# MLP-mixer and grouped attention kernel: w2 copies behind identity and square, slot 1's first layer in a second-layer bank, last weighted sums in column halves

## The chip, the cores and the metric

The kernel runs on one core of one Trainium2 chip, in one launch. The metric is the device time in microseconds, median of the runs. Engines are TensorE (PE; its weight loads are PEld), VectorE (DVE), ScalarE (ACT), GpSimdE (POOL) and SyncE (SP), which issues most DMAs. TensorE writes its products to PSUM, which has eight banks here, each of 128 partitions by 512 float32; the other engines read them out.

## The reference

x has 2048 rows of 448 columns. Two branches read the layer-normalized x, and both are added to x:

```python
xn = _layernorm(x, axis=-1)
return x + _A_ref(xn, A_wq, A_wk, A_wv, A_wo) + _B_ref(xn, B_w1, B_b1, B_w2, B_b2)

# _A_ref: 16 heads of 28 share one key and one value head
q = (x @ wq).reshape(B, S, H, Dh).transpose(0, 2, 1, 3)
k, v = x @ wk, x @ wv
scores = einsum("bhqd,bkd->bhqk", q, k) * (Dh ** -0.5)
o = einsum("bhqk,bkd->bhqd", softmax(scores), v)
return o.transpose(0, 2, 1, 3).reshape(B, S, H * Dh) @ wo

# _B_ref: normalizes once more, then 448 -> 1792 -> 448
y = _layernorm(x, axis=-1)
h = _gelu(einsum("bsd,df->bsf", y, w1) + b1)      # tanh form
return einsum("bsf,fd->bsd", h, w2) + b2
```

## The kernel before

Rows are worked on in four chunks c of 512 (four tiles of 128). The order of the instructions on each engine is written out by hand (the tile framework's manual schedule): generators yield after each matmul, and the loops around them put other work in between. The framework adds the waits. Each engine takes its instructions strictly in that order, so an instruction that waits holds up all behind it.

**Three stages.** To about 66 us: layer norms, projections to q, k and v, query rows stored to DRAM (`qd`). From 66 to about 480 us: the MLP, with the row maxima of the attention scores and the first "turned" scores put in between. Then attention proper, to the end.

**Precision.** Matrices are split into a rounded high part and the remainder (`w1h`, `w1l`; `w2h`, `w2l`; `hh`, `hl`), and a product is three matmuls: high by high, high by low, low by high.

**The MLP in slots.** There are 4 x 14 slots n, one for each chunk c and block ft of 128 of the 1792 hidden columns, and two more to finish. Slot n runs the first layer of block n (`mlp1`, eleven matmuls at lines L179, L182 and L184 into the bank `ph`), and then the second layer of block n - 2 (`mlp2`, twelve matmuls at L625, L628, L631 into four banks `m2_0` to `m2_3`, in which all 14 blocks add up). PSUM is full: three banks `m` for scores, four for the second layer, and only one `ph`.

Behind the first layer follows the gelu. ScalarE reads the bank twice: identity with bias into `hx` (L599) and the scaled square into `hz` (L600); the square's end frees `ph`. GpSimdE makes the tanh's argument (L601, L602). `middle` is ScalarE's tanh (L605) and GpSimdE's last two steps (L606, L607: `hx` is then the gelu). `ending`, which the next slot runs under the name `closing`, rounds it to `hh` on ScalarE (L612) and makes the remainder `hl` on GpSimdE (L614).

These pieces are called between the twelve matmuls of `mlp2`, by a table from the matmul's number to the piece (`stages`). `texp` is an exponential of turned scores (L569). In slots 5, 7, 9, 11, 13 (and so on in later chunks; `norms`) another table also holds the normalization of the next chunk, whose transposes (L271, evacuated to `xh` at L272) use the bank `ph`. Slots 0 and 1 have no `mlp2`: their pieces are called at the slot's end in order of their numbers.

**Splitting w2.** In each odd slot of the first chunk (1, 3, ..., 13) two blocks of w2 are split: `w2_split` at once issues ScalarE's copy into `w2h` (L339), thus ahead of the slot's first layer, identity and square. Its `low` part, a stage, makes `w2l` of one block on VectorE and of the other on GpSimdE (L343), and issues the load of the next raw pair on SP. `w2h` and `w2l` take the space that the projections used, among others for `qe`, from which query rows are stored to `qd` until the MLP begins; the first writes wait for these DMAs.

**Scores in the slots.** After some matmuls a score matmul into an `m` bank is put in: row maxima (L517 on TensorE, reduced by VectorE at L518) or turned scores (L551, read out by VectorE at L552). In the odd slots of the first chunk only row maxima are put in; the even slots begin with four turned ones. There are three `m` banks, so a score matmul waits for VectorE to have read the third one before it.

**The tail.** Attention works in units u (chunk, group of four heads) and key tiles kt. Weighted sums are four matmuls for each kt, one a head, each into 32 partitions of the bank `po` by 512 columns (`pv`, L829). After the last unit's last kt, `end_jobs` runs: nine spins (matmuls of the identity, L396, read by nobody) while VectorE normalizes `po` in two column halves (`shares`: transpose L807, reciprocal L808, transpose L809, product L810), ScalarE and VectorE split the result (`oth` L811, `otl` L812), and TensorE multiplies by the output weights (L741, L742, L743).

Of the kernel before, what the change touches and what calls it, by code (L numbers as in the profile page):

```python
# [15 lines left out]
P = 128  # L16
# [22 lines left out]
def block_kernel(ctx, tc, x, wq, wk, wv, wo, w1, b1, w2, b2, out):  # L39
# [296 lines left out]
    def w2_split(s):  # L336
        raw = wl_q.pop(0)
        ab = slice(2 * s, 2 * s + 2)
        act.activation(w2h[:, ab, :], raw, AF.Copy)  # L339

        def low():
            for eng, b in ((dve, 0), (pool, 1)):
                eng.tensor_sub(w2l[:, 2 * s + b, :], raw[:, b], f(w2h[:, 2 * s + b, :]))  # L343
            if s + 2 < NF // 2:
                w2_load(s + 2)

        return low

    def q_slot(c, i):
        xh, xl = xts[c, False]  # L350
# [43 lines left out]
    def spin(n, t=None):  # L394
        for _ in range(n):
            pe.matmul(idle if t is None else t, ident, ident, start=True, stop=True)  # L396
# [194 lines left out]

    def mlp1(c, ft):
        yh, yl = xts[c, True]
        ph = php.tile([P, CW], F32, name="ph")
        fs = slice(ft * P, (ft + 1) * P)
        yield from proj_steps(ph, lambda b: w1h[:, b, fs], lambda b: w1l[:, b, fs], yh, yl)
        hx = hrp.tile([P, CW], F32, name="hx", bufs=2)
        hz = hrp.tile([P, CW], F32, name="hz", bufs=2)
        act.activation(hx, ph, AF.Identity, bias=b1t[:, ft:ft + 1])  # L599
        act.activation(hz, ph, AF.Square, bias=b1s[:, ft:ft + 1], scale=GELU[0] ** 0.5)  # L600
        pool.tensor_scalar(hz, hz, 1.0, 1.0, op0=ALU.mult, op1=ALU.add)  # L601
        pool.tensor_mul(hz, hz, hx)  # L602

        def middle():
            act.activation(hz, hz, AF.Tanh, scale=GELU[1])  # L605
            pool.tensor_scalar(hz, hz, 0.5, 0.5, op0=ALU.mult, op1=ALU.add)  # L606
            pool.tensor_mul(hx, hx, hz)  # L607

        def ending():
            hh = hrp.tile([P, CW], F32R, name="hh")  # L610
            hl = hrp.tile([P, CW], F32R, name="hl")
            act.activation(hh, hx, AF.Copy)  # L612
            hs[c, ft] = (hh, hl)
            pool.tensor_sub(hl, hx, f(hh))  # L614

        return middle, ending

    def mlp2(c, ft, stages):
        if ft == 0:
            m2s[c] = [m2p.tile([P, D], F32, name=f"m2_{k}") for k in range(CT)]  # L620
        m2 = m2s[c]
        hh, hl = hs.pop((c, ft))
        for k in range(CT):
            ts = slice(k * P, (k + 1) * P)
            pe.matmul(m2[k], hh[:, ts], w2h[:, ft, :], start=(ft == 0), stop=False)  # L625
            stages[3 * k]()
            yield
            pe.matmul(m2[k], hh[:, ts], w2l[:, ft, :], start=False, stop=False)  # L628
            stages[3 * k + 1]()
            yield  # L630
            pe.matmul(m2[k], hl[:, ts], w2h[:, ft, :], start=False, stop=(ft == NF - 1))  # L631
            if ft == NF - 1:
                t = CT * c + k
                a = lines.pop(t)
                dve.tensor_add(a, a, m2[k])
                nc.sync.dma_start(ad[:, t, :], a)
            stages[3 * k + 2]()
            yield

    def slot(n):  # L640
        nonlocal maxed, ending
        middle = low = none
        closing, ending = ending, none
        if n < len(mslots):
            if split(*mslots[n]):
                low = w2_split(n // 2)
            middle, ending = yield from mlp1(*mslots[n])
        texp = turned_exp if n < len(mslots) - 1 else none
        stages = {0: texp, 1: texp, 2: low, 3: closing, 5: middle}
        if n in norms:  # L650
            stages = {4: norms[n], 5: texp, 6: texp, 7: closing, 8: norms[n], 9: middle, 10: low}
        if n >= 2:
            yield from mlp2(*mslots[n - 2], [stages.get(i, none) for i in range(12)])
        else:
            for i in sorted(stages):
                stages[i]()
# [131 lines left out]
        pool.tensor_sub(otl, oc, f(oth))  # L788
        yield

    def end_jobs(u, po):
        while side.step() or oside.step():
            pass
        c, g = units[u]
# [2 lines left out]
        tr, rb, on = att.tile([P, CW], F32, name="tr2", bufs=1), att.tile([P, CW], F32, name="tr", bufs=1), att.tile([P, CW], F32, name="oc", bufs=1)  # L797
        rc = att.tile([P, CW // 32], F32, name="rc", bufs=1)
        last = mtile([P, P])
        spin(9, last)  # L800

        def blocks(t, h):
            return t[:, h].rearrange("p (a b) -> p a b", b=32)
# [17 lines left out]

    pos, ps, pairs = {}, {}, {}

    def pv(u, kt):
        if kt == 0:
            pos[u] = op.tile([P, CW], F32, name="po")
        po = pos[u]
        for j in range(4):
            pe.matmul(po[32 * j:32 * j + 32, :], vs[:, kt, :], ps.pop((u, kt, j)),  # L829
                      start=(kt == 0), stop=(kt == NT - 1))  # L830
        if kt == NT - 1:
            if u == NU - 1:
                end_jobs(u, pos.pop(u))
                return
            side.add(norm_jobs(u, pos.pop(u)))
            side.step()
            c, g = units[u]
            if c < NCH - 1 and g == NG - 1:
                oside.add(o_wait(c, range(NG), range(CT)))
# [36 lines left out]
    for n, (u, kt) in enumerate(steps):  # L876
# [11 lines left out]
        for what in ORDERS[u in TURNED][n % 2]:  # L888
# [21 lines left out]
            elif what == "P":  # L910
                assert not jobs
                for _ in range(BURST if n else 0):
                    pv(*pvq.pop(0))
    while pvq:
        pv(*pvq.pop(0))
    while side.step():
        pass
    while oside.step():
# [24 lines left out]
```

## Time and profile before

| | us |
|---|---|
| median of 3 runs | 1094.62 (1094.16 to 1096.04) |
| profiled execution | 1097.33 |
| its span, first to last instruction | 1095.6 |
| mean granted TensorE clock | 0.996 of full speed |
| TensorE busy | 1080.2 (99%) |
| VectorE busy | 909.2 (83%) |
| ScalarE busy | 736.7 (67%) |
| GpSimdE busy | 561.0 (51%) |

The page has the busy times, the span in 40 equal slices (a digit is a tenth; PEclk is the granted clock of TensorE), the chain of work that ended last, and groups of instructions. The waits view adds up who waited for whom: engine, tile and line, then the releaser; total, times, longest. The timeline view lists instructions in order of time: start, duration, engine, line, operation, output and input tile, and in brackets the idle time before it with what ended that. The windows view gives for a stretch its length, the busy time of TensorE, its weight loads, VectorE, ScalarE and GpSimdE, then the granted clock, the DMA share and GB/s. Tile numbers are left out of names, so `m` stands for score banks and for `m2_0` to `m2_3` alike. TensorE records of float32 matmuls come in pairs, those of the rounded type singly.

### The profile page before, as it was taken

The page shows a single profiled execution, that of the slowest core. Times are in us where ns is not written, and L with a number is a line of the kernel's source. Part 1 is how long each engine was busy: PE and PEld are TensorE (multiplying, and loading weights), DVE is VectorE, ACT ScalarE, POOL GpSimd, SP SyncE. Part 2 cuts the span into 40 slices and gives each one's busy share as a digit, 9 for nine tenths or more (in the row PEclk, how much of TensorE's full clock was granted, in tenths as well). Part 3 has the DMA queues.
Part 4 walks back from the last instruction along what each step waited for, and adds up shares of the span by engine and source line. Part 5 has one row for each costly group of instructions (what it writes and reads, how often), then busy time and mean ns, then how long its engine had stood idle before and what let it go on. Part 6 is the DMA issues. An engine that isn't in the chain of part 4 may idle for free.

```text
span 1095.6 us, 17543 instructions
## 1 busy us (share of the span) xinstructions
PE 1080.2 (99%) x5777; PEld 715.9 (65%) x5777; DVE 909.2 (83%) x1847; ACT 736.7 (67%) x1279; POOL 561.0 (51%) x694
## 2 busy tenths in 40 slices
PE   9989999999999999999999999999999999999998
PEld 8768888888888888865555555555546454555444
DVE  7768899888988998886888997799987898886743
ACT  6765555666666666658777776677775777765783
POOL 6347788768767777764334433433442343343220
PEclk9989999999999999999999999999999999999999
DMA  8675546777877777877977798588796678895720
GB/s 280 206 230 136 137 120 161 196 177 190 209 184 181 192 195 170 216 169 156 204 186 173 182 227 215 129 199 190 181 215 174 174 175 200 199 199 131 182 52 35
DMA packets 140512, 195.15 MB, mean 178 GB/s; under 512 B 17086, under 2 KB 96116, under 8 KB 140420
## 3 DMA queue, kind: packets, MB, share of 16 engines
q1 hardware_dynamic: 127684, 172.11, 62.9%
q0 software_dynamic: 11328, 21.33, 8.7%
q8 instruction: 46, 0.75, 0.3%
q10 hardware_dynamic: 1408, 0.57, 0.2%
q14 instruction: 46, 0.38, 0.1%
HBM read 115.22 MB, written 77.71 MB: 176 GB/s over the span
## 4 chain that ended last, share of the span: by engine, by line
PE 92%; DVE 5%; ACT 1%; issue 1%; DMA 1%; SPq 0%; ACTq 0%; DVEq 0%
PE po L829 22%; PE m L517 18%; PE m L860 17%; PE ph L179 10%; PE m L551 5%; PE m L628 4%; PE m L625 4%; PE m L631 4%; PE m L741 1%; PE ph L182 1%; PE ph L184 1%; PE m L742 1%; PE m L743 1%; DVE mx L518 1%; PE qp L179 1%
## 5 line engine op out<-in xcount | busy, mean ns | idle before, releaser
L518 DVE TENSOR_REDUCE mx<-m 128x1 f32<-128x512 f32 x784 | 506.4, 679 | 80.8 <-PE m L517 71.9
L861 ACT ACTIVATE p<-m 128x512 f32<-128x512 f32 x784 | 402.5, 609 | 163.3 <-PE m L860 163.2
L517 PE MATMUL m<-ks,qm 128*128 128x512 f32 x784 | 322.2, 411 | 0.0
L860 PE MATMUL m<-xh,ks 128*128 128x512 f32 x784 | 258.7, 399 | 0.9 <-DVE half L712 0.9
L829 PE MATMUL po<-p,vs 128*32 128x512 f32 x2048 | 246.0, 598 | 0.0
L517 PEld LDWEIGHTS m<-ks,qm 128*128 128x128 f32 x784 | 147.0, 187 | 117.3 <-ACT p L861 35.4
L860 PEld LDWEIGHTS m<-xh,ks 128*128 128x128 f32 x784 | 144.4, 188 | 51.0 <-ACT p L861 13.6
L552 DVE TENSOR_SCALAR_CACHE_REDUCE raw<-m 128x512 f32<-128x512 f32 x240 | 161.0, 689 | 18.9 <-PE m L551 10.8
L843 DVE STREAM_TRANSPOSE p<-half 128x1024 f32<-128x1024 f32 x120 | 148.2, 1236 | 5.3 <-PE po L829 3.3
L569 ACT ACTIVATE raw<-raw,m 128x1024 f32<-128x1024 f32 x120 | 133.1, 1151 | 0.0
L829 PEld LDWEIGHTS po<-p,vs 128*32 128x32 f32 x2048 | 53.5, 109 | 120.2 <-issue 114.2
L599 ACT ACTIVATE hx<-ph,b1t 128x512 f32<-128x512 f32 x56 | 38.6, 690 | 135.3 <-PE ph L184 128.8
L551 PE MATMUL m<-ks,q 128*128 128x512 f32 x240 | 95.7, 399 | 0.6 <-DVE mx L518 0.6
L614 POOL TENSOR_TENSOR hl<-hx,hh 128x512 fp32r<-128x512 f32 x56 | 72.9, 1302 | 35.3 <-ACT hh L612 35.3
L631 PE MATMUL m<-w2h,hl 128*128 128x448 f32 x224 | 82.8, 369 | 0.3 <-POOL hl L614 0.3
L628 PE MATMUL m<-w2l,hh 128*128 128x448 f32 x224 | 81.6, 364 | 0.0
L625 PE MATMUL m<-w2h,hh 128*128 128x448 f32 x224 | 81.5, 364 | 0.0
L504 POOL DMA_DIRECT2D xh<-mn x15 | 8.1, 543 | 131.5 <-ACT mn L500 131.5
L607 POOL TENSOR_TENSOR hx<-hx,hz 128x512 f32<-128x512 f32 x56 | 72.9, 1302 | 4.7
L602 POOL TENSOR_TENSOR hz<-hz,hx 128x512 f32<-128x512 f32 x56 | 72.6, 1296 | 4.7
L179 PE MATMUL ph<-xh,w1h 128*128 128x512 f32 x168 | 67.2, 400 | 4.6 <-ACT hz L600 4.6
L179 PE MATMUL ph<-xh,w1l 128*128 128x512 f32 x168 | 66.4, 395 | 0.0
(167 smaller groups left out, 1369.5 us busy)
## 6 DMA issues: line engine op xcount, KB each, us to landing
td<-raw SPq DMA_DIRECT2D x240, 256.0 KB
half<-td SPq DMA_DIRECT2D x120, 512.0 KB
xh<-qd POOLq DMA_DIRECT2D x60, 168.0 KB, 4.2
a<-in_A_x_dram SPq DMA_DIRECT2D x32, 224.0 KB
qm<-qd POOLq DMA_DIRECT2D x112, 56.0 KB, 4.4
qd<-qe SPq DMA_DIRECT2D x24, 256.0 KB
qm<-qd SPq DMA_DIRECT2D x84, 56.0 KB
ad<-a SPq DMA_DIRECT2D x16, 224.0 KB
```

Of the source, the lines that this page charges most:

```text
L179: pe.matmul(ps, w, v, start=(n == 0), stop=False)
L517: pe.matmul(pm, qm[:, t * P:(t + 1) * P], ks[:, n * CW:(n + 1) * CW], start=True, stop=True)
L518: dve.tensor_reduce(mx[:, CT * j + t, n:n + 1], pm, axis=AX.X, op=ALU.max)
L551: pe.matmul(sc, q3[i][:, t * P:(t + 1) * P], ks[:, n * CW:(n + 1) * CW], start=True, stop=True)
L552: dve.tensor_scalar(raw[:, :, 4 * n:4 * n + 4, :].rearrange("p r b i -> p b r i"), sc.rearrange("p (b r i) -> p b r i", r=4, i=32), SCALE, ...
L569: act.activation(raw[:, rs], raw[:, rs], AF.Exp, bias=m3[:, 4:5], scale=1.0)
L628: pe.matmul(m2[k], hh[:, ts], w2l[:, ft, :], start=False, stop=False)
L631: pe.matmul(m2[k], hl[:, ts], w2h[:, ft, :], start=False, stop=(ft == NF - 1))
L829: pe.matmul(po[32 * j:32 * j + 32, :], vs[:, kt, :], ps.pop((u, kt, j)), start=(kt == 0), stop=(kt == NT - 1))
L843: dve.transpose(p.rearrange("p k (g j) -> p g k j", j=32), halves[u, kt // 8][:, :, 32 * (kt % 8):32 * (kt % 8) + 64].rearrange("p g (k j) ...
L860: pe.matmul(s, ks[:, kt * P:(kt + 1) * P], qss[u][:, j, :], start=True, stop=True)
L861: act.activation(p, s, AF.Exp, scale=SCALE)
```

## The change

Three things change. (1) `w2_split` no longer issues its copy at once but returns it as a piece of its own, `high`. In slots with a copy and no normalization, slots 1 and 3, the table becomes: `closing`, `high`, `low`, `middle`. In those with a normalization `high` takes stage 5. So the copy comes behind the slot's identity and square. (2) The first layer of slot 1 goes to the bank `m2_3`, whose tile is made 512 wide for that; slot 2's second layer takes it over. (3) The weighted sums that are left at the end, two kt of the last unit, are done for the first 256 columns and then for the other 256, and the spins behind them are six and not nine.

```diff
@@ -336,7 +336,9 @@
     def w2_split(s):
         raw = wl_q.pop(0)
         ab = slice(2 * s, 2 * s + 2)
-        act.activation(w2h[:, ab, :], raw, AF.Copy)
+
+        def high():
+            act.activation(w2h[:, ab, :], raw, AF.Copy)
 
         def low():
             for eng, b in ((dve, 0), (pool, 1)):
@@ -344,7 +346,7 @@
             if s + 2 < NF // 2:
                 w2_load(s + 2)
 
-        return low
+        return high, low
 
     def q_slot(c, i):
         xh, xl = xts[c, False]
@@ -591,7 +593,7 @@
 
     def mlp1(c, ft):
         yh, yl = xts[c, True]
-        ph = php.tile([P, CW], F32, name="ph")
+        ph = m2p.tile([P, CW], F32, name="m2_3") if (c, ft) == (0, 1) else php.tile([P, CW], F32, name="ph")
         fs = slice(ft * P, (ft + 1) * P)
         yield from proj_steps(ph, lambda b: w1h[:, b, fs], lambda b: w1l[:, b, fs], yh, yl)
         hx = hrp.tile([P, CW], F32, name="hx", bufs=2)
@@ -617,7 +619,7 @@
 
     def mlp2(c, ft, stages):
         if ft == 0:
-            m2s[c] = [m2p.tile([P, D], F32, name=f"m2_{k}") for k in range(CT)]
+            m2s[c] = [m2p.tile([P, CW], F32, name=f"m2_{k}")[:, 0:D] for k in range(CT)]
         m2 = m2s[c]
         hh, hl = hs.pop((c, ft))
         for k in range(CT):
@@ -639,16 +641,20 @@
 
     def slot(n):
         nonlocal maxed, ending
-        middle = low = none
+        middle = high = low = none
         closing, ending = ending, none
         if n < len(mslots):
             if split(*mslots[n]):
-                low = w2_split(n // 2)
+                high, low = w2_split(n // 2)
             middle, ending = yield from mlp1(*mslots[n])
         texp = turned_exp if n < len(mslots) - 1 else none
-        stages = {0: texp, 1: texp, 2: low, 3: closing, 5: middle}
+        stages = {0: texp, 1: texp, 3: closing, 5: middle}
+        if high is not none:
+            stages = {0: closing, 1: high, 3: low, 5: middle}
         if n in norms:
-            stages = {4: norms[n], 5: texp, 6: texp, 7: closing, 8: norms[n], 9: middle, 10: low}
+            stages = {4: norms[n], 5: texp, 6: texp, 7: closing, 8: norms[n], 9: middle}
+            if high is not none:
+                stages.update({5: high, 10: low})
         if n >= 2:
             yield from mlp2(*mslots[n - 2], [stages.get(i, none) for i in range(12)])
         else:
@@ -788,7 +794,7 @@
         pool.tensor_sub(otl, oc, f(oth))
         yield
 
-    def end_jobs(u, po):
+    def end_jobs(u, po, halves_of):
         while side.step() or oside.step():
             pass
         c, g = units[u]
@@ -797,7 +803,8 @@
         tr, rb, on = att.tile([P, CW], F32, name="tr2", bufs=1), att.tile([P, CW], F32, name="tr", bufs=1), att.tile([P, CW], F32, name="oc", bufs=1)
         rc = att.tile([P, CW // 32], F32, name="rc", bufs=1)
         last = mtile([P, P])
-        spin(9, last)
+        halves_of(1)
+        spin(6, last)
 
         def blocks(t, h):
             return t[:, h].rearrange("p (a b) -> p a b", b=32)
@@ -821,6 +828,18 @@
 
     pos, ps, pairs = {}, {}, {}
 
+    def pv_last(u, kts):
+        po = pos.pop(u)
+        rest = [(kt, j, ps.pop((u, kt, j))) for kt in kts for j in range(4)]
+
+        def halves_of(i):
+            h = slice(256 * i, 256 * i + 256)
+            for kt, j, p in rest:
+                pe.matmul(po[32 * j:32 * j + 32, h], vs[:, kt, :], p[:, h], start=False, stop=(i == 1 and kt == NT - 1))
+
+        halves_of(0)
+        end_jobs(u, po, halves_of)
+
     def pv(u, kt):
         if kt == 0:
             pos[u] = op.tile([P, CW], F32, name="po")
@@ -829,9 +848,6 @@
             pe.matmul(po[32 * j:32 * j + 32, :], vs[:, kt, :], ps.pop((u, kt, j)),
                       start=(kt == 0), stop=(kt == NT - 1))
         if kt == NT - 1:
-            if u == NU - 1:
-                end_jobs(u, pos.pop(u))
-                return
             side.add(norm_jobs(u, pos.pop(u)))
             side.step()
             c, g = units[u]
@@ -911,8 +927,8 @@
                 assert not jobs
                 for _ in range(BURST if n else 0):
                     pv(*pvq.pop(0))
-    while pvq:
-        pv(*pvq.pop(0))
+    assert pvq and all(u == NU - 1 for u, kt in pvq)
+    pv_last(NU - 1, [kt for u, kt in pvq])
     while side.step():
         pass
     while oside.step():
```

## The prediction

> **What bounds the kernel now.** I read the page first: busy time, the clock row, the chain that ended last.
>
> ```profile
> span 1095.6 us, 17543 instructions
> PE 1080.2 (99%) x5777; PEld 715.9 (65%) x5777; DVE 909.2 (83%) x1847; ACT 736.7 (67%) x1279; POOL 561.0 (51%) x694
> PEclk9989999999999999999999999999999999999999
> PE 92%; DVE 5%; ACT 1%; issue 1%; DMA 1%; SPq 0%; ACTq 0%; DVEq 0%
> ```
>
> TensorE is the bound nearly everywhere, so an edit gains only where TensorE stands still or runs slowly. The clock row has one dip, in the third slice (55 to 82 us). The waits of TensorE say where it stands still; the three that the change can touch:
>
> ```profile
> PE ph L179 <- ACT hz L600: 4.6, 2, 3.6
> PE m L741 <- ACT oth L811: 0.9, 1, 0.9
> PE m L551 <- DVE mx L518: 0.6, 3, 0.2
> ```
>
> The first is the largest wait of TensorE in the whole run: the first layer waits twice for the square to release its only bank. TensorE's timeline shows where: at the starts of slots 1 (70.83) and 2 (78.09). The second layer first runs in slot 2, at 84.14.
>
> ```profile
> 69.36 0.47 PE L551 MATMUL m<-ks,q 128*128 128x512 f32 x1
> 70.83 0.50 PE L179 MATMUL ph<-xh,w1h 128*128 128x512 f32 x1 [1.00 <-ACT hz L600]
> 74.14 0.39 PE L184 MATMUL ph<-xl,w1h 128*128 128x512 f32 x1
> 78.09 0.80 PE L179 MATMUL ph<-xh,w1h 128*128 128x512 f32 x1 [3.57 <-ACT hz L600]
> 83.38 0.46 PE L551 MATMUL m<-ks,q 128*128 128x512 f32 x1
> 84.14 0.36 PE L625 MATMUL m<-w2h,hh 128*128 128x448 f32 x1
> 87.73 0.40 PE L179 MATMUL ph<-xh,w1h 128*128 128x512 f32 x1
> 91.17 0.36 PE L625 MATMUL m<-w2h,hh 128*128 128x448 f32 x1
> ```
>
> Slot 2's first layer takes 84.14 - 78.09 = 6.05 us, slot 3's the same 15 matmuls 91.17 - 87.73 = 3.44 us (0.229 each). The windows view gives the reason in its clock column, the first figure behind the five busy times, before DMA share and GB/s:
>
> ```profile
> 76.00:78.00 2.00, 0.00 (x0) 0.00 (x0) 0.63 (x1) 2.00 (x4) 0.00 (x0) 0.67 0.94 258
> 78.00:80.00 2.00, 1.91 (x5) 1.54 (x6) 0.65 (x2) 0.56 (x2) 1.79 (x2) 0.50 0.36 94
> 83.00:84.00 1.00, 1.00 (x5) 0.81 (x4) 0.59 (x3) 0.00 (x0) 0.92 (x2) 0.75 0.97 367
> ```
>
> A mean of 0.67 over 2 us means the clock fell to half at about 76.7; 0.75 over 1 us means it rose again at 83.5. So the stall costs idle time and then slow matmuls. Together: from 70.83 - 1.00 = 69.83, two first layers at full speed end at 69.83 + 2 x 3.44 = 76.71, but the second layer starts at 84.14. The loss is 7.43 us: 4.57 idle, 2.86 slow clock. This is what the change can win.
>
> Why the square was late, from ScalarE's timeline (L339 is the w2 copy; the columns are start, duration, idle before):
>
> ```profile
> 70.09 0.68 ACT L600 ACTIVATE hz<-ph,b1s 128x512 f32<-128x512 f32 x1
> 72.97 0.63 ACT L605 ACTIVATE hz<-hz 128x512 f32<-128x512 f32 x1
> 75.94 0.95 ACT L339 ACTIVATE w2h<-raw 128x896 fp32r<-128x896 f32 x1 [2.34 <-DMA td<-raw]
> 76.79 0.67 ACT L599 ACTIVATE hx<-ph,b1t 128x512 f32<-128x512 f32 x1
> 77.36 0.68 ACT L600 ACTIVATE hz<-ph,b1s 128x512 f32<-128x512 f32 x1
> ```
>
> ScalarE takes its instructions in order. The copy waits 2.34 us for a DMA (its space held query rows still being stored; the row names a later store), and slot 1's identity and square, ready from 74.5 on, are queued behind it.
>
> **The change part by part.** *Slot 1's bank and the copy's place.* With the first layer of slot 1 in its own bank, slot 1 starts at 69.83 and slot 2 at 73.27; slot 2's bank was released by the square that ended at 70.77. Both waits on L600 go. The second-layer bank is needed again only at slot 2's tenth second-layer matmul, long after. What is late next is the copy: it still has to wait for the DMA, and it now stands behind slot 1's identity and square and slot 0's hh. And hh needs slot 0's gelu, which GpSimdE ends at 74.39 + 1.26 = 75.65:
>
> ```profile
> 74.39 1.26 POOL L607 TENSOR_TENSOR hx<-hx,hz 128x512 f32<-128x512 f32 x1
> 78.83 1.28 POOL L602 TENSOR_TENSOR hz<-hz,hx 128x512 f32<-128x512 f32 x1
> 81.17 1.27 POOL L614 TENSOR_TENSOR hl<-hx,hh 128x512 fp32r<-128x512 f32 x1
> 76.97 0.63 DVE L343 TENSOR_TENSOR w2l<-raw,w2h 128x448 fp32r<-128x448 f32 x1 [1.94 <-ACT w2h L339]
> 79.35 0.69 DVE L552 TENSOR_SCALAR_CACHE_REDUCE raw<-m 128x512 f32<-128x512 f32 x1 [1.75 <-PE m L551]
> 92.02 0.68 ACT L600 ACTIVATE hz<-ph,b1s 128x512 f32<-128x512 f32 x1
> 92.58 0.63 ACT L612 ACTIVATE hh<-hx 128x512 fp32r<-128x512 f32 x1
> ```
>
> hh takes 0.63 (75.7 to 76.33); the copy 0.95, with the 0.1 by which ScalarE's instructions overlap in these rows: 76.25 to 77.2. The DMA had landed by 75.94. Then VectorE's queue: `low` of slot 1 puts its w2l part ahead of slot 2's four score evacuations. It starts 0.08 after the copy and takes 0.63: 77.91. The first evacuation (0.69) ends at 78.6. Three score banks hold three of slot 2's scores, so the fourth waits for that evacuation. It is the 13th matmul of slot 2, due at 73.27 + 12 x 0.229 = 76.02. So TensorE stands still there 2.6 us: a new wait, on VectorE, that before lay inside the old one.
>
> From the last L551 to the second layer took 84.14 - 83.38 = 0.76, so the second layer starts at 78.6 + 0.76 = 79.35 at full clock. hl does not delay it: slot 1's two GpSimdE steps end at about 77.65 and hl 1.27 later at 78.9; its first reader is the fourth matmul of the second layer, some 0.6 after 79.35. Gain: 84.14 - 79.35 = 4.8 us, if the clock stays up.
>
> Does it? The nearest rows are the 1.00 stall, with no low clock behind it, and the 3.57 stall, which cost 2.86. Both ends are kept (0 to 2.86). By a straight line between them 2.6 us costs (2.6 - 1.00) / (3.57 - 1.00) x 2.86 = 1.8, the value I take. Net 3.0 us.
>
> [...]
>
> *Slot 3.* Its copy was queued ahead of the identity; now it follows identity, square and hh. In these rows hh ends at 93.21, so the copy ends at about 94.1. VectorE came to its part of w2l at 92.41, now one reduce later:
>
> ```profile
> 92.41 0.61 DVE L343 TENSOR_TENSOR w2l<-raw,w2h 128x448 fp32r<-128x448 f32 x1
> 92.95 2.51 DVE L518 TENSOR_REDUCE mx<-m 128x1 f32<-128x512 f32 x4
> ```
>
> One reduce is 2.51 / 4 = 0.63, so VectorE waits from 93.0 to 94.15: 1.1 us, with the reduces that free the score banks queued behind it. Three banks cover about two scores, some 0.7 us of it in this stage; I take 0.4 lost, between 0 and 1.1.
>
> *Slots 5 to 13* have the stage lists with the transposes. There the copy follows the xh evacuation, and VectorE's part stays at stage 10:
>
> ```profile
> 136.72 0.60 ACT L272 ACTIVATE xh<-ph 128x512 fp32r<-128x512 f32 x1 [0.75 <-PE ph L271]
> 139.38 1.03 DVE L343 TENSOR_TENSOR w2l<-raw,w2h 128x448 fp32r<-128x448 f32 x1
> ```
>
> The copy ends at 137.3 + 0.95 = 138.25, 1.1 us before VectorE asks for it: nothing. ScalarE's hh and tanh come some 0.85 later, GpSimdE's hl and w2l some 0.75; their readers on TensorE come a slot (about 7 us) later, and that slack hides them. The w2 loads on SP's queue wait for GpSimdE's w2l and shift by the same 0.75, with rows and score stores behind them that are needed slots later. If that cover were gone, each slot would pay up to 0.85. On the other side, w2l took 1.03 here against 0.61 in slot 3, and TensorE waits of 0.2 (the 0.6 in three pieces above) go with it. A shift of GpSimdE may free them: gain 0 to 0.6, I take 0.2.
>
> *The tail.* The last eight weighted sums become sixteen of half the columns, nine spins become six.
>
> ```profile
> 1081.62 3.64 PE L829 MATMUL po<-p,vs 128*32 128x512 f32 x32
> 1085.19 2.27 PE L396 MATMUL m<-ident 128*128 128x128 f32 x18
> 1087.59 0.47 PE L741 MATMUL m<-woh,oth 128*128 128x448 f32 x1
> 1084.22 0.13 PEld L829 LDWEIGHTS po<-p,vs 128*32 128x32 f32 x4 [0.30 <-issue]
> 1085.33 0.45 DVE L807 STREAM_TRANSPOSE tr<-po 128x256 f32<-128x256 f32 x1 [3.91 <-PE po L829]
> ```
>
> The records count two per matmul, so the last eight are 16 records, half of 3.64 us. Were the first half's normalization to start when its columns are done, it would start 0.9 us earlier. But in the changed kernel's built order the first transpose waits for the count that the last of all sixteen matmuls brings, second half included: nothing is uncoupled. What is added is weight loads: 16 more records at 0.13 for four, 0.5 us if none is hidden, 0 if all are, as now (VectorE starts 0.14 after TensorE's next work). I take 0.1 lost, and keep -0.5 to +0.9. Three spins fewer end TensorE's filler 0.76 earlier; L741 waits for ScalarE's oth anyway, and a gap of 0.76 lies below the 1.00 stall that left no low clock.
>
> **Sum.** 3.0 - 0.4 + 0.2 - 0.1 = 2.7 us. All of it passes to the end, as TensorE is 99% busy behind it. The profiled execution took 1097.33 us, 1.73 around its span, and lies 2.71 above the median of 1094.62; 1097.33 - 2.7 = 1094.6 there is 1091.9 on the median.
>
> **The rivals.** *The clock stays up* through the shorter stall. For it: 2.6 is well below 3.57, and the 1.00 stall left no trace. Against it: the clock fell 2.2 us into the old stall. Gain 4.8 - 0.4 + 0.2 - 0.1 = 4.5: 1090.1. [...]
>
> *The low clock lasts as long as before,* 6.8 us (76.7 to 83.5), now all of it under matmuls: 3.4 lost instead of 1.8. Gain 1.1: 1093.5.
>
> *Slower: VectorE waits for the late copy in every odd slot.* If in slots 5 to 13, too, the copy ended 1.75 us after VectorE asks, with 0.75 covered, each of the five would lose 1.0: 2.7 - 5.0 = -2.3, 1096.9. It decides once the copy ends more than 0.75 behind; by the rows it ends 1.1 ahead, so ScalarE would have to be nearly 3 us later than I reckon.
>
> *It does not do what it says:* slot 2 waits for the whole old stall in VectorE's queue, and nothing moves: 1094.6. The old stall ended at 78.09, the new one at 78.6; what speaks against it is that 12 more matmuls are done by then.
>
> **How the numbers follow.** Forecast 0.54 (1091.9), clock up 0.24 (1090.1), long low clock 0.12 (1093.5), slower 0.07 (1096.9), nothing 0.03. A measurement of this kernel tells about 0.2%, 2.2 us, from no change. Faster by more holds the clock-up case and four fifths of the forecast (its own bounds for slot 3 and the clock reach below 2.2): 0.68. Within takes the rest of it, the long low clock and nothing: 0.25. Slower 0.07. The range, 1089.4 to 1094.0, takes in the clock-up case with the 0.6 of the small waits, and on the other side the long low clock with half a microsecond more; it leaves out the last two cases.
>
> **What would show it.** In the changed profile: no wait of L179 on the square; a wait of the score matmul (L551 before) of about 2.6 us on VectorE near 76 to 79, inside slot 2's first layer; the second layer's first matmul near 79.4 and slot 3 near 83 to 85 (87.73 before); a dip of the clock of 3 to 4 us behind the stall (1.8 us lost at half speed is 3.6 us of it), or none; a VectorE idle of about 1.1 before w2l in slot 3; VectorE's first tail transpose still about 0.1 behind the last weighted sum. I am wrong if slot 3 starts later than 86, if w2l waits for the copy in slots 5 to 13, or if the time after slot 4 differs from before by more than half a microsecond.

## The result and the profile after

The changed kernel is slower: 1098.64 us against 1094.39 us, a ratio of 1.0039 with a 95% interval of 1.0026 to 1.0052 (2.8 to 5.7 us). Measured once more beside its parts it was 1.0035 (1.0023 to 1.0046). The forecast was 1091.9.

The profiled execution took 1100.26 us. From its page: the span, TensorE's busy time, the clock row and the shares of the chain that ended last. The clock row no longer shows a dip near the third slice, as the slow stretch (78.2 to 85.1, below) now falls on both sides of that slice's end at 82.4; a new dip stands at the very end.

```profile
span 1098.5 us, 17567 instructions
PE 1081.5 (98%) x5787; PEld 717.5 (65%) x5787; DVE 911.2 (83%) x1847; ACT 736.7 (67%) x1279; POOL 563.2 (51%) x694
PEclk9999999999999999999999999999999999999998
PE 87%; DVE 4%; DMA 4%; ACT 3%; issue 1%; POOL 1%; SPq 1%; DVEq 0%; ACTq 0%
```

TensorE's waits in the changed kernel (line numbers have moved: L551 is L553, L518 is L520, L741 is L747; the columns are total, times, longest):

```profile
PE m L553 <- DVE raw L554: 3.2, 2, 3.0
PE m L553 <- DVE mx L520: 2.5, 6, 0.8
PE m L747 <- ACT oth L818: 1.7, 2, 0.9
```

The 4.6 us of the first layer on the square are gone. In their place stands one wait of 3.0 on VectorE's score evacuation; the wait of the scores on the reduces has grown from 0.6 to 2.5 us.

The timelines of TensorE, ScalarE and VectorE in the changed kernel show the stall as the prediction built it:

```profile
69.94 0.39 PE L179 MATMUL m<-xh,w1h 128*128 128x512 f32 x1
76.66 0.93 ACT L341 ACTIVATE w2h<-raw 128x896 fp32r<-128x896 f32 x1
77.69 0.82 DVE L345 TENSOR_TENSOR w2l<-raw,w2h 128x448 fp32r<-128x448 f32 x1 [3.68 <-DMA td<-raw]
78.43 0.68 DVE L554 TENSOR_SCALAR_CACHE_REDUCE raw<-m 128x512 f32<-128x512 f32 x1
79.18 0.80 PE L553 MATMUL m<-ks,q 128*128 128x512 f32 x1 [2.96 <-DVE raw L554]
80.62 0.57 PE L627 MATMUL m<-w2h,hh 128*128 128x448 f32 x1
```

Slot 1 starts without a wait (69.94), the late copy ends at 77.59, w2l follows (0.82, where 0.63 was reckoned), and the fourth score of slot 2 stands until the first evacuation behind w2l. Then the clock, in the windows view of the changed kernel:

```profile
78.00:80.00 2.00, 0.82 (x2) 0.73 (x3) 2.00 (x6) 0.63 (x1) 2.00 (x3) 0.56 0.54 137
80.00:82.00 2.00, 2.00 (x6) 1.62 (x6) 1.45 (x6) 1.08 (x2) 1.92 (x3) 0.50 0.09 17
82.00:84.00 2.00, 2.00 (x6) 1.73 (x6) 1.04 (x2) 2.00 (x3) 1.92 (x3) 0.50 0.62 212
84.00:86.00 2.00, 2.00 (x8) 1.73 (x8) 1.27 (x2) 1.30 (x3) 1.79 (x2) 0.73 0.26 59
```

It is half from about 78.2 to 85.1: the last 0.9 us of the stall, and 5.9 us under matmuls.

The best ruler for the rest is the first second-layer matmul of each slot. TensorE's rows of it for slots 4 and 14 in the kernel before (slot 3's, 91.17, was shown):

```profile
98.20 0.36 PE L625 MATMUL m<-w2h,hh 128*128 128x448 f32 x1
172.39 0.36 PE L625 MATMUL m<-w2h,hh 128*128 128x448 f32 x1
```

and for slots 3, 4 and 14 in the changed kernel:

```profile
89.68 0.36 PE L627 MATMUL m<-w2h,hh 128*128 128x448 f32 x1
97.74 0.36 PE L627 MATMUL m<-w2h,hh 128*128 128x448 f32 x1
173.63 0.36 PE L627 MATMUL m<-w2h,hh 128*128 128x448 f32 x1
```

From slot 3's row to slot 4's: 98.20 - 91.17 = 7.03 before, 97.74 - 89.68 = 8.06 after, 1.03 lost. From slot 4's to slot 14's: 74.19 before, 75.89 after, 1.70 lost. Slot 3's row came 1.49 earlier; by slot 14 the kernel is 1.24 behind. From slot 14's row to the end of the span it takes 924.87 against 923.21, another 1.66; so 2.90 in all, the difference of the two spans.

### The profile page after: what moved, and what is told of

It reads as the page before. It is cut to its first block, busy times and chain, and to the rows that moved or that the text cites. A ratio compares the mean times of both kernels' runs of the same rounds, so it can differ in the third digit from the quotient of the medians.

```text
span 1098.5 us, 17567 instructions
## 1 busy us (share of the span) xinstructions
PE 1081.5 (98%) x5787; PEld 717.5 (65%) x5787; DVE 911.2 (83%) x1847; ACT 736.7 (67%) x1279; POOL 563.2 (51%) x694
## 4 chain that ended last, share of the span: by engine, by line
PE 87%; DVE 4%; DMA 4%; ACT 3%; issue 1%; POOL 1%; SPq 1%; DVEq 0%; ACTq 0%
PE po L848 21%; PE m L519 17%; PE m L876 17%; PE ph L179 8%; PE m L553 5%; PE m L630 3%; PE m L627 3%; PE m L633 3%; DMA td<-raw 2%; DVE mx L520 1%; PE m L747 1%; PE m L748 1%; PE m L749 1%; ACT raw L571 1%; PE ph L184 1%
## 5 line engine op out<-in xcount | busy, mean ns | idle before, releaser
L520 DVE TENSOR_REDUCE mx<-m 128x1 f32<-128x512 f32 x784 | 506.2, 679 | 81.3 <-PE m L519 72.9
L553 PE MATMUL m<-ks,q 128*128 128x512 f32 x240 | 95.6, 398 | 5.8 <-DVE raw L554 3.2
L488 POOL DMA_DIRECT2D xh<-qd x60 | 38.1, 636 | 52.5 <-PE m L519 40.5
L179 PE MATMUL ph<-xh,w1h 128*128 128x512 f32 x165 | 64.9, 394 | 0.0
```

The source lines that it names most:

```text
L179: pe.matmul(ps, w, v, start=(n == 0), stop=False)
L520: dve.tensor_reduce(mx[:, CT * j + t, n:n + 1], pm, axis=AX.X, op=ALU.max)
L553: pe.matmul(sc, q3[i][:, t * P:(t + 1) * P], ks[:, n * CW:(n + 1) * CW], start=True, stop=True)
```

## The experiments

Each kernel was timed against the kernel before on the same chip; the ratio to it has its 95% interval behind it. The edits are shown in shortened form.

**The parts alone.** *Slot 1 alone*: bank and late copy in slot 1, the rest as before.

```
+ first layer of slot 1 in "m2_3"; n == 1: stages = {0: closing, 1: high, 3: low, 5: middle}
  n > 1: high() at the head of the slot, low where it was; tail as before
```

> Slot 1 alone has the new bank and the late copy; slots 3 to 13 copy at the slot's start and the tail is whole columns, as before. Theory A (the odd slots 3 to 13 eat the gain): the start wins what the two profiles show at slot 3's first matmul, 1.5 us net of the rest, so 1091.5 to 1093.5 beside 1094.4. Rival B (the new stall of 3.0 us in VectorE's queue and the low clock behind it cost in an ordinary execution more than the old stall): 1095.5 to 1098. Rival C (the tail is the loss): like A, 1091 to 1093.

Measured: 0.9992 (0.9983 to 1.0001), 1094.82 us. So slot 1's part is worth about 0.8 us (between 1.9 and nothing), not 3.0.

*Late copies alone*: slots 3 to 13 as changed, slot 1 and the tail as before.

```
+ n == 1: high() at the head of the slot; first layer in its old bank
  n == 3: stages = {0: closing, 1: high, 3: low, 5: middle}
  n in norms: stages.update({5: high, 10: low})
```

> Only slots 3 to 13 have the late copy (slot 3: hh, copy, low, tanh; slots 5 to 13: copy at stage 5). Slot 1, its bank and the tail are as before. Theory A: VectorE's xn and w2l meet GpSimdE's hl, which hh now makes later, and wait for it; with slot 3's wait for the copy that costs 2 to 3.5 us: 1096.5 to 1098. Rival B: nothing there, 1094 to 1095. Rival C: nothing, 1094 to 1095.

Measured: 1.0017 (1.0008 to 1.0026), 1097.30 us. By the ruler: slot 3 takes 8.06, slots 4 to 14 75.44, so 1.03 + 1.25 lost. The whole change lost the same 1.03 and 1.70; the difference is slot 5 (7.04 us here, 7.52 there, 7.03 before).

*The tail alone*, slots as before:

```
- spin(9, last)
+ halves_of(1); spin(6, last)      (halves_of(0) ahead of end_jobs)
```

> Only the tail is changed: the last eight weighted sums in column halves, six spins. Theory A: in the profiles the first transpose and the first output matmul keep their distance to the last sums; at most 1 us more where the clock falls before the last six matmuls: 1094.4 to 1095.4. Rival C (the tail is the main loss, as the spins that are left out let the clock fall in most executions): 1096 to 1098. Rival B: 1094 to 1095.

Measured: 0.9997 (0.9988 to 1.0007), 1094.72 us: not told from nothing.

*Slot 1 with its low half deferred*: as the first, but VectorE's w2l goes out behind slot 2's first second-layer matmul, so that it no longer stands ahead of slot 2's evacuations.

```
- n == 1: stages = {0: closing, 1: high, 3: low, 5: middle}
+ n == 1: stages = {0: closing, 1: high, 5: middle}
+ n == 2: stages[0] = low of slot 1, then turned_exp
```

> As slot1_only, but slot 1's low part (both halves of w2l and the next load) is issued in slot 2 behind its first second-layer matmul, so VectorE reads slot 2's four turned scores first. If the new stall is VectorE's queue, it goes: TensorE waits some 1 us for w2l and hl at the first second-layer block, no low clock, and the second layer starts near 78 and not 80.6: 1088.5 to 1091 by theory A, 1089 to 1091 by B too (B says that the stall is the loss). If the stall has another cause, the same as slot1_only.

Measured: 0.9983 (0.9974 to 0.9991), 1093.00 us, faster than the kernel before, but not the 1088.5 to 1091 expected. TensorE's row of the first second-layer matmul has no long wait ahead of it:

```profile
77.91 0.44 PE L627 MATMUL m<-w2h,hh 128*128 128x448 f32 x1 [0.79 <-issue]
```

So w2l's place in VectorE's queue is what makes the new stall, as the prediction said; it had not asked what the old stall is usually worth. The low clock is not always gone with it: six profiles have this order, and in two of them (the runs with the tail in halves and with the whole change, below) the clock fell for 3.41 us in slot 2 all the same, and slot 2's second-layer row to slot 3's took 10.07 us instead of 8.5.

**The whole again, and where its loss lies.** Up to here the parts summed to less than the whole. *The whole change, unaltered*:

> The whole change, unaltered, beside its parts on one chip. Against the kernel before, slot 1's part alone took -0.8 us, the late copies of slots 3 to 13 alone +1.7, the tail alone about -0.3 (not told from 0): +0.6 if parts add. If an interaction is real, the first comparison repeats: +4.2 (1.0039). Theory of an interaction: slot 2's stall of 2.9 us now lies where it is followed by slow clock, two clock windows instead of one or none, and the tail's clock falls as well; then the mean clock of the runs is 0.997 or less, and each window of 3.41 us at half clock costs 1.7 us. Rival (the first comparison was unlucky): +0.6, mean clock 0.998 to 1.0.

Measured: 1.0035 (1.0023 to 1.0046), 1098.70 us; the first comparison was no accident. *Without the tail's halves*:

```
- pv_last(NU - 1, [kt for u, kt in pvq])
+ while pvq: pv(*pvq.pop(0))      (end_jobs with spin(9, last), as before)
```

> The whole change without the tail's column halves. If the tail has no part in it: the same time as the whole change, within 0.5 us. If the tail's clock drop (six last matmuls of 0.57 instead of 0.37 us) belongs to the column halves: 0.7 to 0.9 us less than the whole change.

Measured: 1.0029 (1.0019 to 1.0038), 1098.29 us: 0.4 us less than the whole change, at the edge of both theories; this alone tells nothing of the tail. *Only slots 5 to 13 late*:

```
+ n in norms: stages.update({5: high, 10: low})    (slots 1 and 3: high() at the head, as before)
```

> The kernel before with only the copies of slots 5 to 13 moved behind the xh evacuation; slots 1 and 3 and the tail as before. Theory (VectorE's xn and w2l and GpSimdE's hl hold each other up, because hl comes later): four to five losses of 0.2 to 0.45, +0.9 to +1.7 us against the kernel before, xn 0.94 in slots 7, 9 and 11. Rival of the prediction (these slots cost nothing): 0 to -0.6.

Measured: 1.0028 (1.0018 to 1.0037), 1098.13 us, so +2.0 to +4.1 us for the part that the prediction had put at a gain of 0.2, and more than the 0.9 to 1.7 expected here. Its profile lost 1.75 us from slot 4's row to slot 14's; that execution was the fastest of its nine, 1.90 below their median. The order differs from the kernel before on ScalarE alone, by the place of five copies (the second-layer tiles are 512 wide here too). *The whole change with the copy behind hh in slots 5 to 13*:

```
- n in norms: stages.update({5: high, 10: low})
+ n in norms: stages[7] = closing, then high;  stages[10] = low
```

> The whole change, but in slots 5 to 13 the copy one place further back, behind hh instead of ahead of it, so that hh and hl keep their old times and only tanh comes later; the copy still ends before VectorE's w2l. Theory (hl's shift is the cause): xn 0.30 again in slots 7 to 11, VectorE waits of the score matmuls in slots 5 to 13 go, 1.2 to 1.7 us less than the whole change. Rival (any delay on ScalarE costs, tanh's too): the same time as the whole change.

Measured: 1.0007 (0.9998 to 1.0016), 1095.90 us: 2.8 us less than the whole change, where 1.2 to 1.7 were expected, by moving one ScalarE instruction past another in each of five slots. Slots 4 to 14 take 170.06 - 96.62 = 73.44, less even than before (74.19):

```profile
96.62 0.36 PE L627 MATMUL m<-w2h,hh 128*128 128x448 f32 x1
170.06 0.36 PE L627 MATMUL m<-w2h,hh 128*128 128x448 f32 x1
```

Why, is to be read in slot 9 on VectorE, GpSimdE and TensorE. Before (L614 makes hl, L263 is a layer-norm piece of 64 columns; w2l, 1.03, was shown):

```profile
134.44 0.36 PE L625 MATMUL m<-w2h,hh 128*128 128x448 f32 x1
138.02 1.30 POOL L614 TENSOR_TENSOR hl<-hx,hh 128x512 fp32r<-128x512 f32 x1
139.16 0.30 DVE L263 TENSOR_SCALAR xn<-a,lnq,lnqb 128x64 f32<-128x64 f32 x1
139.28 0.66 POOL L606 TENSOR_SCALAR hz<-hz 128x512 f32<-128x512 f32 x1
141.07 0.50 PE L551 MATMUL m<-ks,q 128*128 128x512 f32 x1 [0.21 <-DVE mx L518]
```

The changed kernel, with ScalarE's copy ahead of hh:

```profile
134.67 0.36 PE L627 MATMUL m<-w2h,hh 128*128 128x448 f32 x1
137.43 0.95 ACT L341 ACTIVATE w2h<-raw 128x896 fp32r<-128x896 f32 x1
138.27 0.62 ACT L614 ACTIVATE hh<-hx 128x512 fp32r<-128x512 f32 x1
138.97 1.30 POOL L616 TENSOR_TENSOR hl<-hx,hh 128x512 fp32r<-128x512 f32 x1 [0.68 <-ACT hh L614]
139.37 0.95 DVE L263 TENSOR_SCALAR xn<-a,lnq,lnqb 128x64 f32<-128x64 f32 x1
140.24 0.61 DVE L345 TENSOR_TENSOR w2l<-raw,w2h 128x448 fp32r<-128x448 f32 x1
140.24 1.10 POOL L608 TENSOR_SCALAR hz<-hz 128x512 f32<-128x512 f32 x1
141.51 0.50 PE L553 MATMUL m<-ks,q 128*128 128x512 f32 x1 [0.41 <-DVE mx L520]
```

The copy behind hh:

```profile
136.54 1.30 POOL L616 TENSOR_TENSOR hl<-hx,hh 128x512 fp32r<-128x512 f32 x1
137.66 0.31 DVE L263 TENSOR_SCALAR xn<-a,lnq,lnqb 128x64 f32<-128x64 f32 x1
137.89 0.62 DVE L345 TENSOR_TENSOR w2l<-raw,w2h 128x448 fp32r<-128x448 f32 x1
138.44 0.62 POOL L608 TENSOR_SCALAR hz<-hz 128x512 f32<-128x512 f32 x1 [0.60 <-ACT hz L607]
```

In the changed kernel the copy makes hh, and so GpSimdE's hl, later: 4.30 us behind the slot's first second-layer matmul instead of 3.58. hl is now under way when VectorE starts xn, and xn takes 0.95 instead of 0.30: it ends (140.32) with hl (140.27). GpSimdE's next instruction then takes 1.10 instead of 0.62, with w2l beside it. The reduces behind xn come later, and the score matmul waits 0.41 instead of 0.21. Before, the two met as well, but at w2l (1.03 instead of 0.62). With the copy behind hh their rows overlap by no more than 0.2 us and none is longer. By the ruler the slot takes 8.13, 8.34 and 7.68 us in the three kernels.

Slots 7 and 11 are like slot 9 (xn 0.94 in the changed kernel, 0.31 with the copy behind hh; 0.22 and 0.23 lost). In slot 13 w2l takes 1.37 instead of 0.65 beside hl, and the slot loses 0.59. Slot 5 is another case. There hl does not come later, and w2l and hl start within 0.03 us of each other in each kernel; before, hl was the one lengthened (1.79), in the changed kernel w2l was (1.76), and 0.49 us were lost. The changed kernel's second profile lost nothing there and the one with the copy behind hh lost the same 0.49, so the place of the copy does not decide this one.

In slot 9's rows the one of a meeting pair that is lengthened ends after the other (xn at 140.32 behind hl's 140.27, GpSimdE's hz at 141.34 behind w2l's 140.85). What makes it wait is not shown by any run here.

**Slot 3, the old stall, and two better versions.** *The kernel before, profiled again*:

> The kernel before, unaltered, profiled once more on the chip of its variants. The prediction sized slot 1's term from one execution (idle 1.00 and 3.57 us, slow clock 2.86 us). Theory that this execution was an unusual one: the two waits of the first layer on the square are 2.9 to 3.3 us together, and at most one clock window of 3.41 us is slow, so 0 to 1.7 us lost by it; from the start of slot 1 to the first matmul of slot 3 some 2 to 4 us less than the 16.90 of the first profile. Rival (the first execution was typical): 4.6 idle and two slow windows again. Time: as before, ratio 1.000 within 0.001.

Measured: 1.0006 (0.9997 to 1.0015). TensorE's waits and rows:

```profile
PE ph L179 <- ACT hz L600: 3.9, 2, 2.8
71.59 0.50 PE L179 MATMUL ph<-xh,w1h 128*128 128x512 f32 x1 [1.12 <-ACT hz L600]
78.14 0.73 PE L179 MATMUL ph<-xh,w1h 128*128 128x512 f32 x1 [2.82 <-ACT hz L600]
90.31 0.36 PE L625 MATMUL m<-w2h,hh 128*128 128x448 f32 x1
```

Idle 3.94, between the two theories; slot 3's row at 90.31 instead of 91.17. Four of the variants keep the old slot 1 too, so there are six executions of it: slot 3's row came at 91.17, 90.31, 89.72, 88.87, 87.84 and 87.81, a mean of 89.29. The one that the prediction sized its first term from is the latest of the six. Five profiles have the new slot 1: 89.68, 88.56, 88.33, 88.26 and 87.09, a mean of 88.38. The difference is 0.9 us, which is what slot 1's part alone measured. The old stall varies in both its terms: the two waits of L179 add up to 4.57, 3.94, 4.00, 3.27, 3.51 and 2.92 us in that order, and the clock was low behind them for 6.8, 3.4, 3.4, 3.4, 0 and 0 us (mean granted clocks of the six: 0.996, 0.997, 0.997, 0.998, 1.0 and 1.0). The executions as a whole go with it: the two latest rows belong to executions 2.71 and 0.93 above the median of their runs, the two earliest to some 1.90 and 0.46 below theirs.

*Only slot 3 late*:

```
+ n != 3: high() at the head of the slot
  n == 3: stages = {0: closing, 1: high, 3: low, 5: middle}
```

> The kernel before with only slot 3's copy moved behind its identity, square and hh. By the traces of the whole change (slot 3 lost 0.85 to 1.0 us, VectorE waited 0.95 for the copy): +0.85 to +1.0 us. By the prediction: +0.4. Rival (hidden): 0.

Measured: 1.0016 (1.0007 to 1.0024), 1096.33 us. Its ruler loses 1.03 in slot 3 and nothing elsewhere. VectorE's row in it:

```profile
92.64 1.18 DVE L345 TENSOR_TENSOR w2l<-raw,w2h 128x448 fp32r<-128x448 f32 x1 [0.95 <-ACT w2h L341]
```

*Slot 1 deferred (the diff above), slots 3 to 13 as before, tail in halves and six spins*:

> Slot 1's first layer in a second-layer bank, its copy behind identity, square and hh, its low half issued only behind slot 2's first second-layer matmul, slots 3 to 13 as before, and the tail in column halves. Without the tail this took 0.9983 of the kernel before; the tail alone 0.9997. If the parts add: 0.9980, about -2.2 us.

Measured: 0.9995 (0.9984 to 1.0005), 1094.08 us, not the 0.9980 expected. *The same with slots 5 to 13's copy behind hh* (the diff of that run):

> The same as the run with low deferred and the tail in halves, and in slots 5 to 13 the copy behind hh instead of at the head of the slot. Theory (VectorE's w2l and GpSimdE's hz and hx exclude each other in the kernel before as well, w2l 1.03 instead of 0.62 in slots 7 to 11): a further -0.2 to -0.6 us. Rival (the copy in the middle of the slot delays tanh, which costs): 0 to +0.8.

Measured: 0.9987 (0.9977 to 0.9997), 1093.02 us, on the side of its theory: 1.06 us below the last run where 0.2 to 0.6 more were expected, but the intervals overlap. Both profiles lost time in the last matmuls, as the changed kernel had. The windows view of the changed kernel over 3.41 us before the end, and its first and last of the six last projection matmuls:

```profile
1088.58:1091.99 3.41, 1.77 (x7) 1.21 (x8) 2.82 (x8) 0.83 (x2) 0.00 (x0) 1.00 0.00 0
1091.76 0.56 PE L747 MATMUL m<-woh,oth 128*128 128x448 f32 x1 [0.90 <-ACT oth L818]
1093.61 0.57 PE L749 MATMUL m<-woh,otl 128*128 128x448 f32 x1
```

TensorE was busy 1.77 of 3.41 us, then the clock fell (at 1092.02), and the last six took 0.56 to 0.57 instead of 0.36 to 0.47. This happened in three of seven profiles with column halves and six spins, and in none of nine with whole columns and nine spins.

**Which part of the tail, and the stall inside the whole.** *The version with slot 1 deferred and slots 5 to 13 behind hh, with the old tail* (whole columns, nine spins):

> Slot 1's low half deferred into slot 2, slot 3 as before, slots 5 to 13's copy behind hh, and the tail as in the kernel before (whole columns, nine spins). In three of six profiles with the column halves and six spins the clock fell before the last six matmuls (0.57 instead of 0.37 us each, about 1.1 us), in none of eight profiles without them. Theory (the halves and their fewer spins make this drop likelier): 0.4 to 0.8 us less than the same kernel with halves and six spins, so 0.998 to 0.9985 of the kernel before. Rival (the tail is neutral): the same 0.9987.

Measured: 0.9980 (0.9971 to 0.9989), 1093.25 us. *With the halves and nine spins*:

```
- spin(6, last)
+ spin(9, last)
```

> The same with the column halves but nine spins instead of six. If the three missing spins cause the drop: last six matmuls at 0.36 to 0.37 us, time as with the old tail. If the halves themselves do: as with six spins, the drop in about half of the executions.

Measured: 0.9974 (0.9964 to 0.9984), 1092.36 us, the fastest version here; TensorE's last matmul at full speed:

```profile
1085.91 0.36 PE L764 MATMUL m<-woh,otl 128*128 128x448 f32 x1
```

By the windows views below it is the three spins that kept the clock up in this profile. In the traces of the kernel before and of the changed kernel the clock changed only at whole multiples of 3.41 us from its other changes (see the last section). Counted in such a step back from this profile's next fall, at 1088.16, a stretch of 3.41 us ends 0.02 us behind the start of the last six matmuls. In the run with slot 1 deferred, the tail in halves and six spins, one ends at the same place, 0.01 behind. The windows views of the two, nine spins first:

```profile
1081.34:1084.75 3.41, 2.37 (x15) 1.61 (x13) 2.81 (x8) 0.83 (x2) 0.00 (x0) 1.00 0.00 0
1084.06:1087.47 3.41, 1.70 (x9) 0.99 (x7) 2.80 (x8) 0.83 (x2) 0.00 (x0) 1.00 0.00 0
```

With nine spins TensorE was busy for 2.37 us of the 3.41 and the clock stayed; with six for 1.70, and it fell. In their times the two tails are not told apart, as the intervals overlap. *The whole change with slot 1's low half deferred* (the diff of slot 1's second run, nothing else):

> The whole change with one edit: slot 1's low half goes out behind slot 2's first second-layer matmul, so that VectorE's w2l no longer stands ahead of slot 2's score evacuations; copies of slots 3 to 13 and the tail as changed. Theory (the new stall of 2.9 us and the low clock behind it are worth what they were without the other parts, 1.8 us): 1.5 to 2.2 us less than the whole change, 1.0015 to 1.002 of the kernel before. Rival (the stall is made up later): 1.0035 as the whole change.

Measured: 1.0020 (1.0011 to 1.0028), 1097.35 us. Against the whole change's 1.0035 the new stall with its slow clock is worth some 1.6 us there too, though these intervals overlap; it is not the whole loss.

## Why the prediction was wrong, point by point

**The old stall (7.43 us to be won): mis-sized.** The arithmetic was right for its execution, but that was the worst of six, in idle time and in slow clock. (The mark set for it, slot 3 not later than 86, was missed at 86.26 in the profiled execution.) In the mean of the executions above, slot 1's part won 0.9, where the forecast had 3.0. The forecast's new time was close: 91.17 - 3.0 = 88.2 for slot 3's row, against a mean of 88.38. What was wrong is the 91.17 that it started from, against a mean of 89.29. The prediction noted that its execution lay 2.71 above the median and did not draw the conclusion that the excess could lie in this very stall.

**The new stall (2.6): right in place and nearly in size.** It measured 2.94 to 2.96 in five executions, at the matmul and for the reason given. Its price in slow clock is no single value: from the end of the same stall to slot 3's second-layer row it took 7.83, 9.22, 9.40, 9.40 and 10.50 us, so the slow clock cost anything from 0 to 2.7. The mean, 1.4, is near the 1.8 of the straight line. The rival in which the clock stays up is what one of the five shows; the one with the long low clock, 6.8 us of it, is what the profiled execution shows, and it ended on the slow side none the less.

**Slot 3 (0.4, between 0 and 1.1): the upper end.** VectorE waited 0.95 where 1.1 was foreseen. What the step left out is that w2l itself ran into GpSimdE's instruction and took 1.18 instead of 0.61. The reduces behind it so came some 1.5 us later; the banks covered about 0.5 of that, not 0.7, the score matmul of the changed kernel waited 0.76 and the slot lost 1.03:

```profile
92.60 1.18 DVE L345 TENSOR_TENSOR w2l<-raw,w2h 128x448 fp32r<-128x448 f32 x1 [0.95 <-ACT w2h L341]
94.44 0.50 PE L553 MATMUL m<-ks,q 128*128 128x512 f32 x1 [0.76 <-DVE mx L520]
```

**Slots 5 to 13 ("nothing", and a gain of 0.2): the step that failed.** The copy did end before VectorE asked, and hl's readers were covered, as written. But the prediction asked only who reads hl, not what runs beside it. By the ruler the step lost 1.70 in the changed kernel; alone it measured 2.0 to 4.1. Its own row, w2l at 1.03 instead of 0.61, was the trace of such a meeting in the kernel before, and it was read as something that a shift might free. A shift did free it with the copy behind hh (0.75 below before), where hl keeps its place (3.58) and GpSimdE's hz, which w2l had met, comes 5.48 behind the slot's row instead of 4.84. The shift of this change moved the meeting to xn, ahead of the reduces. The 0.49 of slot 5 is the exception said above.

**The rival on the slow side** had the right slots and the right direction (1096.9) by the wrong mechanism: w2l never waited for the copy in slots 5 to 13.

**The tail (0.1 lost): right when the clock stays up.** The sixteen halves took 1.91 us where the eight sums had taken 1.82, and VectorE's first transpose stood 0.13 behind TensorE's next work (0.14 before). Where the clock fell, the last six matmuls took 2.42 us from the first's start to the last's end (1091.76 to 1094.18) instead of 1.53 (1090.04 to 1091.57 before), 0.9 lost. The two gaps before the projections were taken singly, each below the 1.00 stall; the 3.41 us behind which the clock fell hold both.

**The sum by its steps.** -0.9 (slot 1), +1.03 (slot 3), +1.70 (slots 5 to 13) and 3/7 of 0.9 (the tail's clock) make +2.2 us. The two comparisons give 2.5 to 5.0 and 2.8 to 5.7. The direction and over half of the size are accounted for; 0.3 us at the least, and some 1.5 to 2 at the middle values, are not attributed to a place. Part of it lies behind slot 14: from its row to the end of the span the two profiles of the changed kernel take 924.87 and 924.47 us, the two of the kernel before 923.21 and 923.58. That is 1.3 more in the mean, of which the tail's clock, fallen in one of the two, makes 0.45; why the rest was lost is not shown. The copies of slots 5 to 13 are where the timed runs say more (2.0 to 4.1) than their trace (1.75), and the run of all late copies alone says less (0.9 to 2.8) than its own two parts together; that stays open.

## What to carry to other kernels

Before sizing a gain from one profiled execution, ask whether the stall is one that varies: an execution well above the median may hold its excess just there. When an instruction is moved on one engine, list not only the readers of what it delays but what will run at the same time on VectorE and GpSimdE afterwards; a short instruction there took three times its length (xn, 0.30 to 0.95), and the order of two ScalarE instructions in five slots was worth 2.8 us. Filler matmuls that look superfluous may be holding the clock: with the three spins TensorE was busy for 2.37 of 3.41 us and it stayed up, in the run without them for 1.70 and it fell. So count them over the whole stretch between two busy parts.

## What the runs showed of the hardware

- Some VectorE and GpSimdE instructions took longer where they met: xn 0.95 instead of 0.30 beside hl in slot 9 of the changed kernel, and w2l 1.76 instead of 0.61 beside hl in its slot 5, whose rows on VectorE and GpSimdE are these:

```profile
108.36 1.76 DVE L345 TENSOR_TENSOR w2l<-raw,w2h 128x448 fp32r<-128x448 f32 x1
108.36 1.29 POOL L616 TENSOR_TENSOR hl<-hx,hh 128x512 fp32r<-128x512 f32 x1
```

- The clock fell behind stretches in which TensorE was busy for part of the time, and stayed down through a mostly busy one. The windows view of the changed kernel for the two stretches of 3.41 us around the stall:

```profile
74.83:78.24 3.41, 1.39 (x7) 0.81 (x5) 0.56 (x1) 1.99 (x4) 3.33 (x4) 1.00 0.98 234
78.24:81.65 3.41, 2.47 (x6) 2.05 (x7) 2.87 (x10) 1.18 (x3) 3.33 (x4) 0.50 0.24 60
```

TensorE was busy 41% of the first, and the clock then halved; it was busy 72% of the second, and the clock stayed at half for another 3.41 us.
- In the traces of the kernel before and of the changed kernel the changes of the clock lie whole multiples of 3.413 us apart. It was at half for 6.83 us, twice that (76.67 to 83.50, and 78.26 to 85.09), and fell again 1010.35 and 1006.93 us later (at 1093.84 and 1092.02), 296 and 295 times that. In stretches of 3.41 us between these changes, the kernel before shows

```profile
73.25:76.66 3.41, 1.28 (x6) 0.74 (x4) 1.56 (x3) 1.07 (x2) 1.89 (x2) 1.00 1.02 278
76.67:80.08 3.41, 1.99 (x5) 1.62 (x6) 1.32 (x3) 1.89 (x4) 1.87 (x3) 0.50 0.56 168
80.08:83.49 3.41, 3.41 (x10) 2.67 (x9) 1.40 (x4) 0.63 (x1) 3.33 (x5) 0.50 0.31 69
1087.02:1090.43 3.41, 2.38 (x12) 1.52 (x11) 2.82 (x9) 0.83 (x2) 0.00 (x0) 1.00 0.00 0
1090.43:1093.84 3.41, 1.14 (x6) 0.67 (x4) 1.77 (x4) 0.00 (x0) 0.00 (x0) 1.00 0.73 269
```

and the changed kernel

```profile
81.67:85.08 3.41, 3.41 (x10) 2.91 (x10) 2.06 (x3) 3.41 (x5) 3.11 (x4) 0.50 0.42 135
481.04:484.45 3.41, 2.43 (x11) 1.75 (x10) 2.58 (x7) 1.49 (x4) 2.95 (x2) 1.00 0.82 282
```

At full clock it fell behind the stretches in which TensorE was busy for 1.28 and 1.14 us, and in the changed kernel behind those of 1.39 and 1.77 shown above. Behind all others of the two traces from 5.0 and 6.6 us on, where the clock's records begin, it stayed; the least busy are those of 2.38 and 2.43 us shown. At half clock it stayed low behind 1.99 and 2.47 us, and rose behind 3.41 in both.
- The same stall, 2.94 to 2.96 us long, was followed by 6.83 us of low clock in the changed kernel, by 3.4 in three profiles (in the one with the copy behind hh the clock was 0.56 from 80 to 82 us and 0.59 from 82 to 84), and by none in one (the run without the tail's halves, mean granted clock 0.999).
